# Five instead of four of the eight pairs of the first double unit in the seven-product form, with their first-layer weight sums read where they are made and whole weights stored

## The chip, the cores and the metric

The kernel runs on one core of a Trainium2 chip. The metric is device time in microseconds (us), the median of three runs. The engines are PE (TensorE, matrix products), DVE (VectorE), ACT (ScalarE), POOL (GpSimd) and SP (SyncE, which issues every DMA of this kernel); each runs its own instructions in order and waits for the others by semaphores. SBUF is the memory on the chip, PSUM the banks into which PE accumulates, DRAM the memory behind the DMA queues.

## The reference

```python
ret = scores * Dmat                 # scores = q k^T / 8, Dmat[i, j] = gamma_h ** (i - j) for i >= j, 8 heads of 64, 8 x 576 tokens
x = (ret @ v) -> tokens x 512       # 4608 tokens, heads side by side
h = x @ w_in                        # 512 -> 2048 (first layer)
g = np.maximum(h, 0) + np.log1p(np.exp(-np.abs(h)))   # softplus
out = g @ w_out                     # 2048 -> 512 (second layer)
```

The two weight matrices arrive as 64-bit numbers, the rest as 32-bit.

## The kernel before

**Arithmetic.** Every operand of a large matmul is kept as a high part and a rest (HI, LO), and a product is three matmuls (`TERMS`): rest by high, high by rest, high by high. One such matmul is 128x512 with 128 rows contracted.

**Units.** The 4608 tokens are nine units of 512. Unit 0 is the *opening*: a loop over i = 0 to 15, where one of the 16 slices of the hidden dimension is computed (`hidden_mm`, L540, 12 matmuls), goes through softplus, and is added to the output of the slice before (`output_terms`, L569, 12 matmuls). The 32 weight pieces (16 of w_in, 16 of w_out, 512 KB each) are loaded in this loop, two for each i, into five buffers `wst`, and converted in five steps: p (ACT, L637), t (DVE, L644) and b (DVE, L650) join the two words of a 64-bit number into one fp32 number, c (ACT, L665) makes the high part, d (DVE, L670) the rest. After d the next load is issued (`weight_dl`), and a converted w_in piece is stored to DRAM (`split`), because SBUF has no room to keep it. The order of the steps in an iteration is written out by hand (`ORDERS`).

**Double units.** Units 1 to 8 are four double units, s = 0 to 3, each of 2x2 blocks in tokens and halves of the contracted dimension. The hidden dimension is eight *pairs* j of slices. Done plainly, a pair has eight block products (six matmuls each) in the first layer and eight in the second. In the *seven-product form* (Strassen's, in Winograd's order) it has seven of each: `full_pair` makes the seven of the first layer, and the second layer's are spread over `second` and a later phase. This form needs sums of weight blocks, S1 to S4 for each layer, and sums of x blocks (T1, T2, T3, NT4). The weight sums are made once, in the first double unit, by DVE and ACT: `combine_whole` (L729) or `ring_sum` (L738) add high part and rest to the whole number, `combine_blocks` (L756, four 128x256 additions) makes the sums, `combine_head` (ACT, L760) and `combine_rest` (DVE, L764) split them again, and SP stores them to `combined` (first layer) or `outcombined` (second layer). `whole_out` (L743) makes the whole second-layer weights. From then on all blocks, plain ones and sums, come back from DRAM through a ring of eight buffers, 256 KB a time (`block_load`); `product` (L914) pops one and asks for the next.

**The first double unit** (s = 0) is mixed: pairs 0 to 3 (`MIXED`) have the seven-product form, pairs 4 to 7 (`PLAIN`) are done plainly, as eight *plain slots* (`plain_slot`) for its left half of tokens ahead of the mixed pairs (u = 1) and eight for the right half behind them (u = 2). While the first slots run, weight sums for the mixed pairs are made; in the slots of u = 2 and at the beginning of s = 1, those for pairs 4 to 7. What helpers run in which place is written out in tables of one-letter names (`FIRST_WORK`, `PAIR_WORK`, `SECOND_WORK`, `SUM_WORK`).

**Retention.** Tokens are handled in 36 chunks; one *chunk group* on PE is some 112 to 128 matmuls of 64x64 (`chunk_products`, L236, L252, L340, L352). `GROUPS` puts them into the opening, and the slots and pairs take one each. DVE then scales the values (L294, L498), and helpers add up the T blocks (L506, L517 to L520, L525). `pad()` puts no-ops on PE behind some matmuls, so that instruction blocks end where the chunk groups do (`PADS`).

## Time and profile before

| | |
|---|---|
| median of three runs | 809.93 us (808.10 to 810.88) |
| the profiled execution | 808.64 us, of which the span from first to last instruction 806.9 us |
| PE busy | 800.3 us, 99%, 7228 matmuls, granted clock 1.000 |
| DVE busy | 563.1 us, 70% |
| ACT busy | 398.4 us, 49% |
| DMA | 216.78 MB, 269 GB/s mean |
| the chain that ended last | PE 95%, DMA 3%, DVE 1% |

The opening lasts from about 28 to 120 us of the span, the first slots to 167, the mixed pairs to about 237, the second slots to 286, and the second double unit begins at about 311. Busy shares are means over stages with different limits, so the windows and waits below are taken for one stage each. PE works in a pipeline: the duration of one matmul in a row is longer than the time from one to the next, so that its price is read from the length of a run of many.

### The profile page before, as it was taken

Reading aid. Unit: us, or ns where it says so; the run is one execution under the profiler, and the core shown is the slowest. Engines: PE = TensorE matmul, PEld = TensorE weight load, DVE = VectorE, ACT = ScalarE, POOL = GpSimd, SP = SyncE. Lnnn points to the kernel's source line nnn. Section 1 sums busy time; section 2 is a strip of 40 time slices with the busy share of each in tenths; the row PEclk is TensorE's granted clock in tenths of the full one; section 3 lists DMA queues with packets and bytes.
Section 4 is the critical chain, followed back from the end, with each engine's and each line's share of the span. In section 5 each row is a group of like instructions: output and inputs, shape, how many; then the busy total and the mean of one; then the engine's idle time right before and its main releaser. Section 6 shows DMA issues by size and latency. Waiting matters only on the chain.

```text
span 806.9 us, 19514 instructions
## 1 busy us (share of the span) xinstructions
PE 800.3 (99%) x7228; PEld 659.3 (82%) x7228; DVE 563.1 (70%) x955; ACT 398.4 (49%) x698; POOL 114.1 (14%) x210
## 2 busy tenths in 40 slices
PE   8999999999999999999999999999999999999998
PEld 6788888878888888888888888888888888888887
DVE  5988968688679986667579964546579933224785
ACT  6877763344534363343445644343355734435553
POOL 4322132211221310122111001111100000000000
PEclk9999999999999999999999999999999999999999
DMA  9999879998996779897987678777656775666674
GB/s 358 381 328 331 304 265 381 319 355 292 367 353 214 278 268 395 281 326 255 316 270 234 217 244 258 230 250 252 213 181 218 221 247 192 195 191 194 195 219 159
DMA packets 100458, 216.78 MB, mean 269 GB/s; under 512 B 11152, under 2 KB 11408, under 8 KB 100368
## 3 DMA queue, kind: packets, MB, share of 16 engines
q1 hardware_dynamic: 100368, 215.54, 78.9%
q8 instruction: 62, 1.02, 0.5%
q14 instruction: 28, 0.23, 0.1%
HBM read 174.60 MB, written 40.89 MB: 267 GB/s over the span
## 4 chain that ended last, share of the span: by engine, by line
PE 95%; DMA 3%; DVE 1%; SPq 0%; issue 0%; DVEq 0%
PE sum L1050 20%; PE acc L914 18%; PE third L914 11%; PE two L914 9%; PE two L1050 6%; PE y L569 5%; PE y L580 5%; PE h L540 5%; PE third L252 2%; PE acc L1050 2%; PE third L1050 2%; PE y L1050 2%; PE two L236 2%; PE two L340 2%; PE two L352 2%; DMA wst<-w 1%
## 5 line engine op out<-in xcount | busy, mean ns | idle before, releaser
L1044 DVE TENSOR_TENSOR parts<-g,parts 128x512 fp32r<-128x512 f32 x196 | 134.9, 698 | 138.3 <-ACT parts L1040 135.7
L1050 PE MATMUL sum<-parts,ring 128*128 128x512 f32 x708 | 170.9, 392 | 0.0
L1040 ACT CAST parts<-g 128x512 fp32r<-128x512 f32 x196 | 121.1, 622 | 74.2 <-DVE parts L1044 28.1
L914 PE MATMUL acc<-xt,ring 128*128 128x512 f32 x624 | 156.8, 389 | 0.0
L1050 PEld LDWEIGHTS sum<-parts,ring 128*128 128x128 f32 x708 | 131.6, 188 | 27.8
L914 PEld LDWEIGHTS acc<-xt,ring 128*128 128x128 f32 x624 | 117.0, 188 | 24.4
L914 PE MATMUL third<-xt,ring 128*128 128x512 f32 x408 | 102.7, 389 | 0.0
L914 PEld LDWEIGHTS third<-xt,ring 128*128 128x128 f32 x408 | 76.5, 188 | 16.4 <-DVE s L330 0.3
L914 PE MATMUL two<-xt,ring 128*128 128x512 f32 x336 | 85.7, 390 | 0.7 <-DVE xt L525 0.7
L914 PEld LDWEIGHTS two<-xt,ring 128*128 128x128 f32 x336 | 62.9, 188 | 14.6 <-DVE xt L525 1.1
L229 POOL TENSOR_TENSOR qv<-qv,consts_sb 128x256 f32<-128x256 f32 x58 | 43.4, 748 | 152.9 <-DMA qv<-others 152.9
L1082 ACT COPY acc<-third 128x512 f32<-128x512 f32 x28 | 16.0, 570 | 97.0 <-PE third L914 97.0
L1050 PE MATMUL two<-parts,ring 128*128 128x512 f32 x216 | 50.4, 389 | 0.0
L580 PE MATMUL y<-g,wout 128*128 128x512 f32 x192 | 47.6, 395 | 0.0
L1050 PEld LDWEIGHTS two<-parts,ring 128*128 128x128 f32 x216 | 40.5, 188 | 8.5
L1069 ACT ACTIVATE g<-g 128x512 f32<-128x512 f32 x56 | 35.1, 627 | 23.3 <-DVE g L1102 22.7
L540 PE MATMUL h<-xt,win 128*128 128x512 f32 x192 | 46.1, 390 | 0.0
L569 PE MATMUL y<-wout,g 128*128 128x512 f32 x180 | 44.0, 393 | 0.0
L1125 ACT ACTIVATE g<-acc 128x512 f32<-128x512 f32 x28 | 16.7, 598 | 55.2 <-PE acc L914 55.2
L540 PEld LDWEIGHTS h<-xt,win 128*128 128x128 f32 x192 | 35.9, 188 | 7.7 <-ACT xt L476 0.2
L580 PEld LDWEIGHTS y<-g,wout 128*128 128x128 f32 x192 | 35.4, 188 | 7.9 <-DVE g L555 0.3
L569 PEld LDWEIGHTS y<-wout,g 128*128 128x128 f32 x180 | 33.3, 188 | 7.4 <-ACT g L551 0.3
(168 smaller groups left out, 1262.2 us busy)
## 6 DMA issues: line engine op xcount, KB each, us to landing
ring<-split SPq DMA_DIRECT2D x116, 256.0 KB, 4.4
ring<-combined SPq DMA_DIRECT2D x112, 256.0 KB, 3.5
ring<-outcombined SPq DMA_DIRECT2D x112, 256.0 KB, 3.1
ring<-outsplit SPq DMA_DIRECT2D x84, 256.0 KB, 3.5
qv<-others SPq DMA_DIRECT2D x58, 320.0 KB, 5.3
wst<-w SPq DMA_DIRECT2D x32, 512.0 KB, 6.5
keys<-others SPq DMA_DIRECT2D x58, 256.0 KB, 5.2
split<-win SPq DMA_DIRECT2D x16, 512.0 KB, 6.3
```

The lines of the kernel that those rows point to most:

```text
L229: nc.gpsimd.tensor_mul(v, v, f.unsqueeze(2).broadcast_to([P, 4, D]))
L236: nc.tensor.matmul(L["S"][rows[t], h, part[s]], L["k"][rows[h], s, part[t]], L["q"][rows[h], s, part[t]], start=True, stop=True, skip_grou ...
L252: mm = nc.tensor.matmul(L["T"][rows[h ^ s], t, part[s]], L["kp"][rows[t], s, rows[h]], L["v"][rows[t], s, rows[h]], start=True, stop=True, ...
L540: nc.tensor.matmul(h, tile_of(wins[p], a, kt), xt[:, b, T1 + half, kt % 2], start=(n == 0), stop=(n == 3 * NKT - 1))
L569: nc.tensor.matmul(ys[u][tt], g[:, a, tt * P:(tt + 1) * P], wouts[p][:, :, b], start=p == 0 and n == 0, stop=False)
L580: nc.tensor.matmul(ys[u][tt], tile_of(wouts[p], a, tt), g[:, b], start=u == 1 and p == 2 * MIXED and n == 0, stop=n == 2, skip_group_check ...
L914: nc.tensor.matmul(bank, w[:, ta, kt * P:(kt + 1) * P], xt[:, tb, x, kt], start=start and k == 0, stop=k == 5, skip_group_check=True)
L1040: nc.scalar.copy(t[:, HI], g_slot(J, n))
L1044: nc.vector.tensor_sub(t[:, LO], g_slot(J, n), t[:, HI].bitcast(F32))
L1050: nc.tensor.matmul(bank[m], w[:, a, m * P:(m + 1) * P], t[:, b], start=start and n == 0, stop=n == 2, skip_group_check=True)
L1069: nc.scalar.activation(c, c, AF.Softplus)
L1125: nc.scalar.activation(c21, acc, AF.Softplus)
```

## The change

`PLAIN` goes from 4 to 3: pairs 0 to 4 now have the seven-product form in the first double unit, and six slots are left ahead of them and six behind.

- A permutation `PLACE` decides which buffer and which piece a pair has: the mixed pairs take pieces 6 to 15, and pieces 0 to 5 are the plain ones.
- In the opening, step b writes the joined numbers of a piece side by side, and for the ten w_in pieces of the mixed pairs SP stores them whole (`split_whole`, 256 KB each, right behind b). `combine_load` reads these back instead of high part and rest, so that `combine_whole` is not needed for pairs 0 to 4.
- The first-layer sums of pairs 0 to 4 are written into tiles `direct`, in the SBUF places of the next pair's second-layer weights, and PE reads them there (`product(..., here=...)`) in s = 0. They are stored to `combined` too, for the later double units.
- The first-layer sums of pairs 5 to 7 are made in s = 1 (`load_there`, `combine_whole_of`, `split_store`) and no longer from the ring in the slots of u = 2.
- One chunk group moves from the slots of u = 1 into the opening (`CHUNKS`, `GROUPS`); the work tables and the pads are written anew.

```diff
-PLAIN = 4
+PLAIN = 3
 MIXED = NJ - PLAIN
+PLACE = [(p + 2 * PLAIN) % NF for p in range(NF)]
...
-GROUPS = {1: (4, None), 4: (5, 4), 8: (6, 5), 12: (7, 6), 15: (8, 7)}
-ODD = 12
+GROUPS = {1: (4, None), 4: (5, 4), 7: (6, 5), 10: (7, 6), 13: (8, 7), 15: (9, 8)}
+ODD = 10
+RING_AT = 13
...
+    split_whole = {PLACE[p]: dram.tile([P, 2, HPIECE], F32, name=f"splitwhole{p}") for p in range(2 * MIXED)}
...
-        nc.vector.scalar_tensor_tensor(hi, hi, 3, lo, op0=ALU.logical_shift_left, op1=ALU.bitwise_or)
+        nc.vector.scalar_tensor_tensor(joined(wl[n]), hi, 3, lo, op0=ALU.logical_shift_left, op1=ALU.bitwise_or)
+        p, second = PIECES[n]
+        if not second and p in split_whole:
+            nc.sync.dma_start(split_whole[p], halves(wl[n]))
+
+    def joined(piece):
+        return piece.rearrange("p c a -> p (c a)")[:, 0:PIECE]
...
-            nc.sync.dma_start(f[a], split[2 * j + a].bitcast(F32))
+            nc.sync.dma_start(f[a][:, :, HI], split_whole[PLACE[2 * j + a]])
...
-    def product(bank, x, start=False):
-        w = coming.pop(0)
+    def product(bank, x, start=False, here=None):
+        w = coming.pop(0) if here is None else here
...
-        block_load()
+        if here is None:
+            block_load()
...
+        def sum_here(b):
+            return None if s else direct[J][(b - S1) // 2][:, b % 2]
+
         product(y, B11, True)
         nc.scalar.copy(acc, y)
-        product(z, T1, True)
+        product(z, T1, True, sum_here(S1))
...
-        product(acc, T2)
+        product(acc, T2, here=sum_here(S2))
...
-        product(acc, T3)
+        product(acc, T3, here=sum_here(S3))
...
-        product(z, B22)
+        product(z, B22, here=sum_here(S4))
...
+    def load_there(j, *at):
+        raws[j] = [blocks_in(spare[n]) for n in at]
+        for a, f in enumerate(raws[j]):
+            queued.append(lambda a=a, f=f: nc.sync.dma_start(f, split[PLACE[2 * j + a]].bitcast(F32)))
...
+    def sums_place(j, a):
+        if a not in direct.setdefault(j, {}):
+            p = PLACE[2 * j + 2 + a]
+            place, tag = (wout_pools[p], f"w{p}") if j < MIXED - 1 else (later["quad"], "quad")
+            direct[j][a] = blocks_in(place.tile([P, 2, T], F32R, tag=tag, name="direct"))
+        return direct[j][a]
+
+    def sums_head(j, a):
+        nc.scalar.copy(sums_place(j, a)[:, :, HI], raws[j][a][:, :, LO])
+
+    def sums_rest(j, a):
+        to = sums_place(j, a)
+        nc.vector.tensor_sub(to[:, :, LO], raws[j][a][:, :, LO], to[:, :, HI].bitcast(F32))
+
+    def sums_store(j, a):
+        nc.sync.dma_start(sums_dram[j][a].bitcast(F32), sums_place(j, a).bitcast(F32))
...
-    blocks = schedule((0, prepare_ring, 4, 0, 2))
-    rings = schedule((0, prepare_ring, 4, 2), *[(2 * j - 1, prepare_ring, 4 + j) for j in range(1, 4)])
     for p in range(2 * PLAIN):
         group = groups.pop() if p % 2 else None
-        plain_slot(2, p, B12, B22, group, blocks.get(p, ()), rings.get(p, []) + work_of(SECOND_WORK[p]))
+        plain_slot(2, p, B12, B22, group, (), work_of(SECOND_WORK[p]))
```

The first place is SP in the middle of the opening, about i = 6 to 9: `wst<-w` are the loads of weight pieces, `split<-win` the stores of converted ones. Before:

```order
L627 DMA wst<-w 128x1024 x2
L675 DMA split_116<-win_877 128x1024
L627 DMA wst<-w 128x1024 x2
L675 DMA split_117<-win_956 128x1024
L627 DMA wst<-w 128x1024 x2
```

The same stretch of the change:

```order
L634 DMA wst<-w 128x1024
L660 DMA splitwhole_126<-wst 128x512
L634 DMA wst<-w 128x1024
L688 DMA split_116<-win_850 128x1024
L634 DMA wst<-w 128x1024
L660 DMA splitwhole_127<-wst 128x512
L634 DMA wst<-w 128x1024
L688 DMA split_117<-win_906 128x1024
```

Between the two loads of an iteration now stands a store that reads a `wst` buffer, so that this buffer comes free when the store has landed.

The second place is DVE at the end of the first slots, where it makes the last x sums (L517 to L520, then L525 into `xt`), which the first mixed pair's second product waits for. L555 is the rest of g of the last slot, L756 and L764 weight sums. Before:

```order
L756 TENSOR_TENSOR quad<-quad 128x256 x4
L506 TENSOR_TENSOR xt<-xs,xt 128x2x128
L517 TENSOR_TENSOR xs<-xs 128x2x128
L518 TENSOR_TENSOR t_2659<-xs 128x256
L519 TENSOR_TENSOR xs<-xs 128x2x128
L520 TENSOR_TENSOR xs<-xs,t_2659 128x2x128
L764 TENSOR_TENSOR quad<-quad 128x2x256 x2
L555 TENSOR_TENSOR g<-ab,g 128x512
L525 TENSOR_TENSOR xt<-xs,xt 128x6x128
L525 TENSOR_TENSOR xt<-t_2659,xt 128x2x128
```

The same rows of the change (all line numbers are larger, L562 for L555, L532 for L525):

```order
L513 TENSOR_TENSOR xt<-xs,xt 128x2x128
L524 TENSOR_TENSOR xs<-xs 128x2x128
L525 TENSOR_TENSOR t_2344<-xs 128x256
L526 TENSOR_TENSOR xs<-xs 128x2x128
L527 TENSOR_TENSOR xs<-xs,t_2344 128x2x128
L562 TENSOR_TENSOR g<-ab,g 128x512
L532 TENSOR_TENSOR xt<-xs,xt 128x6x128
L532 TENSOR_TENSOR xt<-t_2344,xt 128x2x128
```

The four additions and the two subtractions of weight sums no longer stand ahead of the last x sums.

The third place is DVE right behind, in the first mixed pair: L743 makes whole second-layer weights of the next pair, L1102 the addition that the pair's c22 needs. Before:

```order
L729 TENSOR_TENSOR quad<-quad 128x2x256 x2
L743 TENSOR_TENSOR quad<-wout_176 128x2x256
L743 TENSOR_TENSOR quad<-wout_177 128x2x256
L756 TENSOR_TENSOR quad<-quad 128x256 x8
L1102 TENSOR_TENSOR g_2733<-acc,g_2733 128x512
```

The change (L755 for L743, L1126 for L1102, L1330 the rest of a sum in its `direct` place):

```order
L768 TENSOR_TENSOR quad<-quad 128x256 x2
L776 TENSOR_TENSOR quad<-quad 128x2x256 x2
L768 TENSOR_TENSOR quad<-quad 128x256 x4
L776 TENSOR_TENSOR quad<-quad 128x2x256
L755 TENSOR_TENSOR quad<-wout_504 128x2x256
L755 TENSOR_TENSOR quad<-wout_505 128x2x256
L1330 TENSOR_TENSOR direct<-quad,direct 128x2x256
L768 TENSOR_TENSOR quad<-quad 128x256 x2
L776 TENSOR_TENSOR quad<-quad 128x2x256
L1126 TENSOR_TENSOR g_2418<-acc,g_2418 128x512
```

The whole weights now stand behind nine rows of sums and splits, and four more operations stand between them and the addition for c22.

## Rows read from the trace of the kernel before

**Rows 1.** Windows: engines' busy us (instructions), PEclk, DMA share, GB/s.
```profile
20.00:40.00 20.00, 19.65 (x140) 15.57 (x138) 18.67 (x36) 16.71 (x30) 6.59 (x10) 1.00 1.00 380
40.00:60.00 20.00, 20.00 (x192) 16.58 (x191) 17.71 (x32) 15.89 (x30) 5.48 (x9) 1.00 0.94 336
60.00:80.00 20.00, 20.00 (x208) 16.59 (x207) 16.38 (x30) 15.71 (x29) 4.03 (x7) 1.00 0.93 322
80.00:100.00 20.00, 20.00 (x208) 16.58 (x207) 18.18 (x33) 15.05 (x28) 2.96 (x6) 1.00 0.86 303
100.00:120.00 20.00, 20.00 (x192) 16.56 (x191) 13.49 (x22) 14.25 (x26) 6.27 (x10) 1.00 0.80 273
...
340.00:360.00 20.00, 20.00 (x192) 16.59 (x191) 11.93 (x21) 9.40 (x17) 3.06 (x6) 1.00 0.95 325
```

**Rows 2.** The chain in order of time: start us, us, what (opening).
```profile
31.17 2.72 PE h L540 x12
...
44.93 0.20 PE third L252
...
46.95 2.95 PE y L569 x12
```

**Rows 3.** The chain: second slots, and the beginning of s = 1.
```profile
238.39 2.95 PE y L580 x12
241.34 1.60 PE y L1050 x6
...
286.46 2.91 PE y L580 x12
...
312.55 1.65 PE two L914 x6
```

**Rows 4.** Timeline of PE at the first mixed pair: start us, us, operation.
```profile
168.90 0.61 PE L914 MATMUL two<-xt,ring 128*128 128x512 f32 x2
170.21 1.19 PE L914 MATMUL two<-xt,ring 128*128 128x512 f32 x4 [0.69 <-DVE xt L525]
```

**Rows 5.** Timeline of DVE ahead of that product.
```profile
166.97 1.29 DVE L764 TENSOR_TENSOR quad<-quad 128x512 fp32r<-128x512 f32 x2
168.18 0.69 DVE L555 TENSOR_TENSOR g<-ab,g 128x512 fp32r<-128x512 f32 x1
168.78 1.37 DVE L525 TENSOR_TENSOR xt<-xs,xt 128x768 fp32r<-128x768 f32 x1
```

**Rows 6.** Timeline of ACT: the high part of that g.
```profile
167.01 0.62 ACT L551 CAST g<-ab 128x512 fp32r<-128x512 f32 x1
```

**Rows 7.** Timeline of DVE in the first mixed pair.
```profile
174.72 0.69 DVE L743 TENSOR_TENSOR quad<-wout 128x512 f32<-128x512 f32 x1 [1.26 <-DMA outcombined<-quad]
...
179.69 0.69 DVE L1102 TENSOR_TENSOR g<-acc,g 128x512 f32<-128x512 f32 x1 [1.10 <-PE acc L914]
```

**Rows 8.** DVE lines by form: busy us, mean ns, idle us before them.
```profile
L756 DVE TENSOR_TENSOR quad<-quad 128x256 f32<-128x256 f32 x64 | 27.1, 445 | 1.2
...
L644 DVE TENSOR_SCALAR wst<-wst 128x512 int32<-128x512 uint32 x32 | 15.3, 482 | 0.3 <-DMA wst<-w 0.3
...
L729 DVE TENSOR_TENSOR quad<-quad 128x512 f32<-128x512 f32 x8 | 6.2, 812 | 0.0
```

**Rows 9.** DMA issues: KB each, median us to landing.
```profile
combined<-quad SPq DMA_DIRECT2D x16, 512.0 KB, 4.1
outcombined<-quad SPq DMA_DIRECT2D x16, 512.0 KB, 6.1
```

**Rows 10.** Timelines of ACT, PE and DVE in the opening.
```profile
85.73 0.62 ACT L551 CAST g<-ab 128x512 fp32r<-128x512 f32 x1 [0.29 <-DVE ab L547]
...
87.35 2.88 PE L569 MATMUL y<-wout,g 128*128 128x512 f32 x12
...
86.99 0.69 DVE L670 TENSOR_TENSOR win<-wst,win 128x512 fp32r<-128x512 f32 x1
...
88.72 0.69 DVE L670 TENSOR_TENSOR wout<-wst,wout 128x512 fp32r<-128x512 f32 x1 [0.70 <-ACT wout L665]
```

More of the change, by code (lines that the diff above doesn't have):

```diff
@@ L43 @@
 STEPS1 = 14
-CHUNKS = 9
+CHUNKS = 10
 FIRST_HALF = NF // 2
@@ L91 @@
 SPLITS = 4
-SEQUENCE = tuple((k, J) for k, js in ((2, range(4)), (1, range(2)), (3, range(4)), (1, range(2, 4)), (4, range(4)))
-                 for J in js)
+SEQUENCE = tuple((k, J) for k, js in ((2, range(MIXED)), (1, range(2)), (3, range(MIXED)), (1, range(2, MIXED)),
+                                      (4, range(MIXED))) for J in js)
 LATE = 7
@@ L579, in output_mm @@
             if u:
-                nc.tensor.matmul(ys[u][tt], tile_of(wouts[p], a, tt), g[:, b], start=u == 1 and p == 2 * MIXED and n == 0,
+                nc.tensor.matmul(ys[u][tt], tile_of(wouts[PLACE[p]], a, tt), g[:, b], start=u == 1 and p == 2 * MIXED and n == 0,
                                  stop=n == 2, skip_group_check=True)
@@ L681, in weight_dl, with pair_blocks @@
             weight_store(n)
-    def pair_blocks(j):
-        blocks = [(j, b) for b in ORDER_PAIR]
+    def pair_blocks(j, kinds=ORDER_PAIR):
+        blocks = [(j, b) for b in kinds]
         return blocks[:-1] + [(j - 1, A12, True)] * (j > 0) + blocks[-1:] + [(j, A11, True)]
     plain = [(j, b) for j in range(MIXED, NJ) for b in range(A22 + 1)]
-    order = plain + [x for j in range(MIXED) for x in pair_blocks(j)]
-    for j in range(MIXED):
-        order += plain[j * 4:j * 4 + 2] + [(MIXED - 1, A12, True)] * (j == 0)
-        order += plain[j * 4 + 2:j * 4 + 4] + [(j, PHASE[0][0], True)]
+    order = plain + [x for j in range(MIXED) for x in pair_blocks(j, (A11, A12, A22))]
+    for p in range(2 * PLAIN):
+        order += plain[2 * p:2 * p + 2] + [(MIXED - 1, A12, True) if not p else (p - 1, PHASE[0][0], True)]
     order += [(J, PHASE[k][0], True) for k, J in SEQUENCE]
@@ L880, in retention_softplus_ffn @@
                 block_load()
+        for j in STORES.get(i, ()):
+            p = PLACE[2 * j]
+            nc.sync.dma_start(wout_dram[2 * j][:, 0].bitcast(F32), wouts[p][:, 0].bitcast(F32))
+            nc.sync.dma_start(wout_dram[2 * j + 1].bitcast(F32), wouts[p + 1].bitcast(F32))
         if i:
@@ L951, in plain_slot @@
             scale_values(k)
-        if u == 2 and p % 2:
+        if u == 2 and p:
             second(ys[2][:2], t)
@@ L956, in plain_slot @@
         outputs_of(u, 2 * MIXED + p)
-    raws = {}
+    raws, direct = {}, {}
     def prepare(j):
@@ L1229, in start, with combine_whole_of, split_store @@
         combined_x([tmps[i][:, n] for n in range(4)], column(i), nc.vector)
+    def load_there(j, *at):
+        raws[j] = [blocks_in(spare[n]) for n in at]
+        for a, f in enumerate(raws[j]):
+            queued.append(lambda a=a, f=f: nc.sync.dma_start(f, split[PLACE[2 * j + a]].bitcast(F32)))
+    def combine_whole_of(j):
+        combine_whole(raws[j])
+    def split_store(j):
+        combine_split(raws[j])
+        for where, f in zip(sums_dram[j], raws.pop(j)):
+            queued.append(lambda where=where, f=f: combine_store([where], [f]))
     def whole_there(j, at):
@@ L1352, in retention_softplus_ffn @@
             if s == FULL:
-                job(divmod(13, NJ), start, 1)
+                for i in range(2):
+                    job(divmod(2 + 11 * i, NJ), start, i)
             else:
```

76 lines of the change are left out of this document (44 added, 32 removed), and 3 rows, old and new, of the table PAIR_WORK.

## The prediction

> **What bounds the kernel now.** I read the busy time by windows first, then the chain, and then the timelines of the engines around the few places where PE does not run through. In the windows PE stands at 20.00 us of 20 from 40 us on [rows 1], and the chain lies on PE for 95% of the span, so what PE has to do is nearly all of the time. What a matmul costs is read from the chain: twelve of 128x512 take 2.72 us [rows 2], so 0.227 us each. PE loses time in two ways only. One is small and regular: a chunk group takes 2.02 us from its first matmul to the next large one, and the run of twelve behind it 2.95 in place of 2.72 [rows 2]; the same 2.95 stands behind a group in a slot [rows 3]. A group costs about 2.25 us wherever it stands, so moving one from the slots into the opening changes nothing by itself. The other way is a late x sum or weight sum, which DVE makes. At the first mixed pair two of six matmuls ran at 168.90, the third was due 0.45 later at 169.35 and came at 170.21, with DVE named as the releaser: 0.86 us lost [rows 4]. Runs that are longer than their matmuls need stand at 241.34 (1.60 for 1.36), 286.46 (2.91 for 2.72) and 312.55 (1.65 for 1.36) [rows 3]: 0.24, 0.19 and 0.29. Together 1.6 us can be had from late DVE work, no more.
>
> **The change part by part.**
>
> *Matmuls.* A plain pair has eight products of six matmuls in each layer, a seven-form pair seven. One pair changes form in one double unit: 2 x 6 = 12 matmuls fewer, at 0.227 [rows 2] **-2.7 us**. PE is the chain there, so this is saved in full if nothing else comes late. Reading a sum in `direct` instead of in a ring buffer changes only an address for PE: at 0, between these bounds: nothing at the low end, and one late first weight load, which I price with the later waits. 21 ring loads of 256 KB that fall away are SP and DMA work; no PE wait on them is in the rows, so 0.
>
> *The last x sums.* Before, L555 stands behind the second of two L764 and begins at 168.18; L525 begins 0.60 later [rows 5]. L555 needs the high part that ACT ends at 167.01 + 0.62 = 167.63 [rows 6]. With the weight sums moved ahead or behind, L555 can begin at 167.65 and L525 at 168.25, 0.5 us earlier. The loss of 0.86 becomes about 0.35. It can't be worse than before by this edit, and at best, with L525 shorter than the 1.37 of its row, nothing is lost: -0.3 to -0.86, taken as **-0.5**.
>
> *DVE in the second slots.* For pairs 4 to 7 sixteen ring sums, sixteen L756 and eight L764 leave these slots: at 0.445 for the 256-wide ones [rows 8] and 0.645 for L764 (two take 1.29) [rows 5], 32 x 0.445 + 8 x 0.645 = 19 us. The three late runs of 0.24, 0.19 and 0.29 stand there or right behind [rows 3]. They are 0.72 us in all; since pair 4's own sums come into the first unit at the same time, I take most, not all: **-0.6** (0 to -0.72). What is moved comes back in s = 1: six L729 at 0.81, twelve L756, six L764, less the second-layer work of pair 4, is 14 - 4.5 = 9.6 us of DVE. In s = 1 DVE was busy 11.93 of 20 us [rows 1], and the pairs of s = 1 take some five such windows, so 8 us of idle time a window cover it: 0. Without this cover it would cost up to 9.6.
>
> *The opening's stores.* Ten stores of 256 KB and one more group's loads (two steps of 576 KB) come into the opening, 3.8 MB. SP issues each between the two weight loads of an iteration, and the buffer that it reads is free only when it has landed. So loads that went out behind the d step of a w_in piece (DVE L670, ends 86.99 + 0.69 = 87.68) go out behind that of the w_out piece (88.72 + 0.69 = 89.41) [rows 10]: 1.7 us later at the worst. Before, DVE waited 0.3 us for these loads over all 32 [rows 8]. Of a late load PE sees nothing up to 1.0 us, because the high part of g is done at 85.73 + 0.62 = 86.35 and PE takes it at 87.35 [rows 10]; in an iteration with a chunk group there are 2.25 us more. That leaves up to 0.7 us in each iteration without a group near it, of which the new `GROUPS` leaves three (5, 8 and 11): 0 to 2.1, taken nearer to the row of 0.3, as **+0.5**.
>
> *Waits on stores behind the first pairs.* In pair 0 the whole second-layer weights of the next pair take buffers that the stores to `outcombined` read. Before, L743 waited 1.26 us there for such a store, and behind it L1102 still waited 1.10 us for PE [rows 7]: the wait was covered. In the change four more operations stand between the two, about 0.6 + 0.45 x 2 + 0.6 = 2.1 us, and the pair begins earlier against a store that takes a median of 6.1 us to land [rows 9]. Behind L1126 PE waits with the pair's last product but one. Below: the cover of 1.10 less 1.26 kept as it is, 0; above: 1.26 + 2.1 - 1.10 - 0.6 (earlier sums) = 1.7. I take **+0.4**. In the same way the tiles `direct` of pair 2 lie where pair 3's g is written: ACT's first copies of pair 3 wait until the two 512 KB stores of these sums have landed, 4.1 us after their issue [rows 9], and they go out at the end of pair 2, with the last six matmuls of pair 2 and twelve of pair 3 ahead of the copy, 18 x 0.227 = 4.1 us. The two are equal; behind a late copy stand the next products' banks. 0 to +1, taken as **+0.3**.
>
> [...]
>
> **Sum.** -2.7 - 0.5 - 0.6 + 0.5 + 0.4 + 0.3 = -2.6 us. The profiled execution of 808.6 (span 806.9) becomes 806.0; the median of the runs lay 1.3 above the profiled one, so 809.9 - 2.6 = **807.3**.
>
> **Rivals.**
> A, the forecast, **807.3**, 805.6 to 808.7 by its terms.
> B, *the waits on stores eat the gain*: both at their upper ends and the opening at 0.5, -2.7 - 1.1 + 0.5 + 1.7 + 1.0 = -0.6: **809.3**. For it: before, DVE already waited at these very stores; against it: it waited with cover.
> C, *the opening becomes bound by its transfers*, on the other side. Three iterations with one group take PE 6 x 2.72 + 2.25 = 18.6 us. They now move 3 x (3 x 512 + 256) KB and 1152 KB of steps, 6.7 MB: 360 GB/s, where the windows show 336, 322 and 303, and 380 in the one window in which the queue was full, share 1.00 [rows 1]. At 380 the stage is fed in 17.6 us. If stores and loads with their waits for buffers only reach 322, three iterations take 20.8 us, 2.2 more, and ten iterations 7.3 us more: -2.7 - 1.1 + 7.3 = +3.5, **813.4**. It decides for slower at about 328 GB/s. Against it: PE was at 20.00 in these windows, so their rates were what was asked for, not what could be had.
> The Trainium skill's page DMA: Bandwidth & Descriptors (Specifications) names about 358 GB/s as the limit of one core's memory; by that the stage would stand just at its bound and rival C would be likelier than I make it. The trace disagrees in one window, with 380.
> D, *all waits vanish*: -2.7 - 0.86 - 0.72 = -4.3, **805.6**.
> That the product count is other than said can't be: the program's rows are written out.
>
> **How the numbers follow.** A 0.48, B 0.23, C 0.18, D 0.11. A difference under 0.3%, 2.4 us, cannot be told from no change in this kernel; 807.5 is that bound, so A stands only just on the faster side, and I give a quarter of A to no change. Faster: 0.36 + 0.11 + a little of B = 0.49; same: 0.12 + 0.2 + a little of C = 0.35; slower 0.16. The range goes from below D, 804.9, into C, 812.0: it leaves out half of C and a little of D.
>
> **What the profile would show.** Right: 7216 matmuls; DVE windows of the second slots clearly below 20; the wait on x sums under 0.4; PE at 20.00 in the opening. Wrong: PE y or h rows over 2.72 in iterations without a group, released by ACT or DVE behind `wst`, with the DMA share at 1.0 (C); PE waits behind L1126 or ACT's copies in pairs 0 and 3 with a store as the releaser (B); or DVE at 20 of 20 in s = 1 with x or weight sums late there. A stall of over 1 us at a place that I name nowhere would make the whole sum wrong.

## The result, and the profile after

The changed kernel takes 815.32 us in the median of seven runs (811.86 to 816.39), the kernel before 809.74 (808.10 to 810.88): a ratio of 1.0065, 95% interval 1.0045 to 1.0084. It is slower by 0.65%. 807.3 was forecast, so 8 us are to be found.

The page of the changed kernel: the span, and busy us, share and instructions of each engine.

```profile
span 813.6 us, 19170 instructions
## 1 busy us (share of the span) xinstructions
PE 802.0 (99%) x7216; PEld 658.2 (81%) x7216; DVE 557.4 (69%) x942; ACT 398.8 (49%) x704; POOL 118.8 (15%) x210
```

The twelve matmuls are gone (7228 to 7216), and yet the span has grown by 6.7 us. The windows of the changed kernel (columns as in [rows 1]) show in which stages PE stood still:

```profile
40.00:60.00 20.00, 20.00 (x192) 16.58 (x191) 17.42 (x31) 15.69 (x30) 5.26 (x8) 1.00 0.94 327
60.00:80.00 20.00, 20.00 (x208) 16.59 (x207) 16.38 (x29) 13.05 (x26) 5.37 (x8) 1.00 0.95 332
80.00:100.00 20.00, 19.10 (x202) 15.28 (x201) 16.93 (x31) 16.02 (x30) 5.23 (x8) 1.00 0.96 344
100.00:120.00 20.00, 19.58 (x308) 16.12 (x307) 14.09 (x25) 12.85 (x23) 5.41 (x10) 1.00 0.98 353
...
200.00:220.00 20.00, 18.41 (x268) 14.76 (x270) 13.23 (x26) 7.54 (x14) 3.76 (x8) 1.00 0.85 299
...
260.00:280.00 20.00, 20.00 (x302) 16.80 (x292) 13.29 (x22) 5.24 (x9) 4.94 (x10) 1.00 0.47 158
...
340.00:360.00 20.00, 17.14 (x174) 13.60 (x173) 14.67 (x27) 6.28 (x11) 3.73 (x7) 0.96 1.00 363
360.00:380.00 20.00, 20.00 (x203) 16.43 (x203) 12.22 (x23) 8.73 (x16) 3.14 (x7) 0.95 0.81 270
```

Against [rows 1] the opening is fuller (344 and 353 GB/s for 303 and 273) and PE no longer runs through in it; PE misses 1.6 us at 200 to 220; and at 340 to 360, at the beginning of s = 1, it misses 2.9 us and its granted clock is below 1 there and in the next window. The second slots, where DVE work was taken out, are as forecast: DVE 13.29 of 20, where the same window of before had 19.72:

```profile
260.00:280.00 20.00, 20.00 (x191) 16.33 (x189) 19.72 (x36) 7.76 (x12) 5.84 (x8) 1.00 0.78 283
```

For a sum I went through PE's rows in order of their starts. Each large matmul should begin 0.227 us behind the one before, or 2.34 us where a chunk group lies between; whatever is more is lost. The usual restart of about 0.11 us behind a group stays in these figures. A loss counts in the stage in which the matmul ahead of it began. In us, by stage of the profiled execution:

```
                        opening  first slots  mixed pairs  second slots  pairs of s=1
                         40-120    120-168      168-240      240-290       315-440
before                     0.45       0.49         1.67         0.71          0.89
after                      2.52       1.20         2.79         0.50          6.47
e1_join_behind_group       4.31       1.22         4.72         0.51          2.96
e2_no_moved_loads          2.26       1.84         4.96         0.51          1.19
e3_spread                  2.30       1.45         4.57         0.51          2.96
e4_no_whole_stores         0.97       0.82         4.94         0.51          7.42
e5_pads_moved              3.42       1.52         1.78         0.50          4.80
e6_stores_early            1.58       1.69         3.49         0.51          3.90
f2_spread_pads_early       2.67       1.24         2.41         0.51          7.14
f3_no_whole_weights        0.96       2.35         5.45         0.51          6.63
f4_spread_no_waits         2.19       1.86         1.90         0.50          1.33
f5_opening_inputs_earlier  1.91       1.85         1.07         0.51          1.45
f6_last_inputs_earlier     1.64       4.72         1.02         0.50          1.57
f7_orders_moved...         0.96       3.61         1.10         0.51          2.27
f8_repaired                1.26       0.92         4.65         0.51          1.45
f9_orders_only             1.28       2.13         2.54         0.51          4.29
f10_repaired_ring_early    1.50       1.30         2.32         0.51          1.45
f11_stores_in_middle       1.37       1.11         0.61         0.50          1.33
```

Between before and after this is +2.1, +0.7, +1.1, -0.2 and +5.6, together +9.3; less the 2.7 of the matmuls that gives 6.6 of the 6.7 us by which the span grew. Each row is one execution, and executions differ: seven of the changed kernel by 4.5 us, seven of the kernel before by 2.8, and 29 of the kernel before, run beside f8, f9 and f10, by 5.4 (807.72 to 813.10). Stages that an edit does not touch show the spread: the last column is 3.9 to 7.4 in the five kernels that have the changed kernel's s = 1 unaltered (after, e4, e5, e6, f9). So a column is compared where an edit acts and against this spread, and times by their ratios.

**The beginning of s = 1.** The chain of the changed kernel there, in order of time:

```profile
348.81 7.56 DMA quad<-split
356.37 0.02 issue
356.40 0.04 DVE quad L741
356.43 0.57 issue
357.01 0.43 DVE u L328
357.44 0.02 issue
357.46 0.43 DVE s L339
357.89 0.04 issue
357.94 2.47 PE third L931 x6
360.41 2.15 PE two L931 x6
362.56 1.36 PE acc L931 x6
```

A 512 KB load of the moved work takes 7.56 us to land. DVE's join of it (L741) waits for it, and behind the join, in DVE's own order, stand L328 and L339 (the two DVE rows of the chain), which read a chunk group's result out of the bank `third`. PE's next product needs that bank. So a transfer that nobody needs for another pair stops PE for 2.1 us. Then six matmuls take 2.47 and 2.15 us in place of 1.36. The granted clock in these microseconds:

```profile
357.00:358.00 1.00, 0.06 (x1) 0.06 (x1) 0.97 (x4) 0.00 (x0) 0.40 (x1) 1.00 1.02 416
358.00:359.00 1.00, 1.00 (x4) 0.81 (x5) 1.00 (x3) 0.00 (x0) 0.62 (x1) 0.76 1.01 395
359.00:360.00 1.00, 1.00 (x4) 0.80 (x3) 0.93 (x4) 0.00 (x0) 0.00 (x0) 0.50 1.04 399
360.00:361.00 1.00, 1.00 (x3) 0.77 (x3) 0.66 (x2) 0.51 (x1) 0.00 (x0) 0.50 0.66 256
361.00:362.00 1.00, 1.00 (x4) 0.74 (x3) 0.00 (x0) 0.06 (x1) 0.00 (x0) 0.54 0.69 235
362.00:363.00 1.00, 1.00 (x6) 0.83 (x5) 0.00 (x0) 0.41 (x1) 0.00 (x0) 1.00 0.96 287
```

After its stop PE runs at 0.50, the lower of its two levels, for some 3.5 us, and eight matmuls lose 0.2 us each.

That DVE was not short of time is seen in one window of 53 us over the first pairs of s = 1. Before:

```profile
312.00:365.00 53.00, 52.98 (x589) 43.34 (x591) 33.51 (x59) 21.84 (x38) 8.76 (x16) 1.00 0.93 317
```

and after:

```profile
312.00:365.00 53.00, 50.10 (x533) 39.99 (x532) 33.17 (x58) 19.47 (x34) 8.46 (x16) 0.97 0.97 353
```

In this window DVE is as busy as before (33.17 and 33.51 us); it stands in front of transfers. Over all pairs of s = 1 (315 to 440 us) it is busy for 88.8 of 125 us, 86.4 before.

**The other places.** The waits of PE in the whole changed kernel (us in total, times, longest):

```profile
PE third L931 <- DVE s L339: 2.1, 1, 2.1
PE third L259 <- issue: 2.1, 2, 1.4
...
PE third L931 <- DVE s L337: 0.7, 1, 0.7
...
PE third L259 <- POOL qv L236: 0.4, 1, 0.4
...
PE acc L931 <- ACT g L1113: 0.2, 1, 0.2
```

The longer of the two stops in the second row lies inside the chunk group of the third mixed pair, with nothing that PE waits for; the other, 0.7 us ahead of a group of the opening at 82.5 us, has no releaser in the trace either. In PE's timeline of the changed kernel:

```profile
203.67 0.22 PE L359 MATMUL two<-qv,s 64*64 64x64 f32 x1
205.28 0.21 PE L259 MATMUL third<-qv,keys 64*64 64x64 f32 x1 [1.39 <-issue]
```

An instruction transfer (queue q8, 16 KB) had begun at 203.01, 0.85 us behind the group's first matmul, and ended at 203.89, 1.39 us before PE went on. In the opening, ACT and DVE wait for weight loads:

```profile
ACT wst L644 <- DMA wst<-w: 3.9, 2, 2.3
...
DVE wst L651 <- DMA wst<-w: 3.0, 6, 0.9
```

which was 0.3 us for DVE before [rows 8]. And ACT's first copy of the fourth mixed pair waits for the store of a sum, in its timeline:

```profile
212.07 0.59 ACT L1108 COPY g<-two 128x512 f32<-128x512 f32 x1 [2.50 <-DMA combined<-direct]
```

### The profile page after: what moved, and what is told of

Its sections match the earlier page's. It is cut to its first block, busy times and chain, and to the rows that moved or that the text cites. A ratio compares the mean times of both kernels' runs of the same rounds, so it can differ in the third digit from the quotient of the medians.

```text
span 813.6 us, 19170 instructions
## 1 busy us (share of the span) xinstructions
PE 802.0 (99%) x7216; PEld 658.2 (81%) x7216; DVE 557.4 (69%) x942; ACT 398.8 (49%) x704; POOL 118.8 (15%) x210
## 4 chain that ended last, share of the span: by engine, by line
PE 85%; DMA 8%; DVE 2%; ACT 2%; issue 1%; SPq 1%; POOL 0%; DVEq 0%; ACTq 0%; POOLq 0%
PE sum L1069 19%; PE acc L931 16%; PE third L931 11%; PE two L931 9%; PE two L1069 7%; PE y L587 4%; DMA wst<-w 3%; PE y L1069 2%; PE third L1069 2%; PE acc L1069 2%; PE third L259 2%; PE y L576 2%; PE two L243 2%; PE h L547 2%; PE two L347 2%; DMA quad<-split 2%
## 5 line engine op out<-in xcount | busy, mean ns | idle before, releaser
L1063 DVE TENSOR_TENSOR parts<-g,parts 128x512 fp32r<-128x512 f32 x203 | 137.7, 690 | 135.4 <-ACT parts L1059 132.9
L1059 ACT CAST parts<-g 128x512 fp32r<-128x512 f32 x203 | 125.4, 622 | 77.5 <-DVE parts L1063 26.6
L931 PE MATMUL acc<-xt,ring 128*128 128x512 f32 x558 | 140.5, 389 | 0.0
L931 PEld LDWEIGHTS acc<-xt,ring 128*128 128x128 f32 x558 | 104.6, 188 | 22.2 <-DVE g L1126 0.4
L931 PE MATMUL two<-xt,ring 128*128 128x512 f32 x288 | 74.1, 393 | 0.0
L931 PEld LDWEIGHTS two<-xt,ring 128*128 128x128 f32 x288 | 54.7, 190 | 12.0 <-DVE held L1315 0.4
L1069 PE MATMUL two<-parts,ring 128*128 128x512 f32 x234 | 54.5, 389 | 0.0
L1069 PEld LDWEIGHTS two<-parts,ring 128*128 128x128 f32 x234 | 43.9, 188 | 9.1
L259 PE MATMUL third<-qv,keys 64*64 64x64 f32 x816 | 34.5, 222 | 2.5 <-issue 2.1
L259 PEld LDWEIGHTS third<-qv,keys 64*64 64x64 f32 x816 | 28.5, 134 | 10.1 <-issue 8.8
```

What stands on the lines that cost most here:

```text
L259: mm = nc.tensor.matmul(L["T"][rows[h ^ s], t, part[s]], L["kp"][rows[t], s, rows[h]], L["v"][rows[t], s, rows[h]], start=True, stop=True, ...
L931: nc.tensor.matmul(bank, w[:, ta, kt * P:(kt + 1) * P], xt[:, tb, x, kt], start=start and k == 0, stop=k == 5, skip_group_check=True)
L1059: nc.scalar.copy(t[:, HI], g_slot(J, n))
L1063: nc.vector.tensor_sub(t[:, LO], g_slot(J, n), t[:, HI].bitcast(F32))
L1069: nc.tensor.matmul(bank[m], w[:, a, m * P:(m + 1) * P], t[:, b], start=start and n == 0, stop=n == 2, skip_group_check=True)
```

## The experiments

Times are medians; ratios are to the kernel before, run on the same chip beside each experiment (its median lay between 808.83 and 809.25 us there, and at 809.74 beside the changed kernel). So two kernels are compared by their ratios; 0.1% is 0.8 us.

### The moved sums in s = 1

**e1_join_behind_group** moves three calls from a place ahead of the chunk group to one behind it:

```diff
-  (("in", 0), combine_whole_of, 5), ... (("in", 1), combine_whole_of, 6), ... (("in", 2), combine_whole_of, 7)
+  (("end", 0), combine_whole_of, 5), ... (("end", 1), combine_whole_of, 6), ... (("end", 2), combine_whole_of, 7)
```

> Only the place of six joins of high part and rest (pairs 5 to 7, second double unit) on DVE changes: behind the chunk group's operations, not ahead of them. In the changed kernel PE loses 6.5 us in the pairs of s = 1 (0.9 before), 2.3 and 0.9 of them where PE's first product of a pair waits for DVE to read the bank third, and DVE waits there for the 512 KB loads that the joins read. Theory (DVE stands in the join, waiting for a load, ahead of work that PE needs): the loss falls by 4 to 5 us, 815.3 becomes 810 to 811.5. Rival 1 (the DMA queue is full there, ring loads come late whatever stands behind them): falls by 1 to 2 us at most. Rival 2 (the 10 us of DVE work that came into s = 1 are too much): no change.

812.71 us, ratio 1.0049 (1.0033 to 1.0065). The loss in s = 1 falls from 6.5 to 3.0, below the spread of 3.9 to 7.4; by the ratio the time falls by 0.16%, 1.3 us, and the intervals overlap (1.0045 to 1.0084 for the changed kernel). The waits at the bank `third` are gone. The gain is below the theory's 4 to 5 because, behind the group, the joins still wait (3.09 us for pair 5's load) and DVE comes late to the addition for c22 (L1126, 0.8 us of PE); it is as late there, 0.65 to 0.94 us, in e4, e5, e6 and f9, whose s = 1 is unaltered.

**e2_no_moved_loads** leaves the loads out:

```diff
 def load_there(j, *at):
     raws[j] = [blocks_in(spare[n]) for n in at]
-    for a, f in enumerate(raws[j]):
-        queued.append(lambda a=a, f=f: nc.sync.dma_start(f, split[PLACE[2 * j + a]].bitcast(F32)))
```

> Leaves out the six loads of 512 KB in s = 1 (the sums of pairs 5 to 7 are then made from whatever lies in the buffers), all DVE, ACT and store work of the moved sums stays. Theory and rival 1 (the loads, by the wait of the join or by filling the queue): loss in the pairs of s = 1 at most 1.5 us, 809.5 to 811. Rival 2 (DVE work): loss stays at 5 to 6.5, 814 to 816.

811.41 us, ratio 1.0034 (1.0021 to 1.0047), 0.31% or 2.5 us below the changed kernel, and 1.2 us lost in s = 1, near the 0.9 of before. The median lies 0.4 above the range that was expected. Its window of the first pairs:

```profile
312.00:365.00 53.00, 52.98 (x557) 43.53 (x556) 36.01 (x63) 21.33 (x38) 8.51 (x15) 1.00 0.93 313
```

DVE is busier (36.01) than in the changed kernel and PE runs through. Rival 2, too much DVE work, is out.

**e3_spread** begins the moved sums in pairs 0, 2 and 4 in place of 0, 1 and 2, joins behind the groups:

> The moved sums of pairs 5, 6, 7 begin in pairs 0, 2 and 4 of s = 1 in place of 0, 1 and 2, with the second-layer sums between them, and the joins stand behind the chunk group. Theory: about the time of the kernel with the joins behind the group alone (810 to 811.5), since the queue was not the limit. Rival 1 (full queue): 2 us or more below that kernel, with DMA share in 320 to 365 us below 0.95 in place of 0.96 to 1.04. Rival 2 (DVE work): somewhat better than the changed kernel, 812 to 814.

812.79 us, ratio 1.0045 (1.0028 to 1.0062): as e1, with the same 3.0 us lost in s = 1; both medians lie 1.2 to 1.3 us above the range that was expected. The queue was hardly less crowded than in e1 (DMA share 0.97 in 320 to 365 us, 1.00 in e1, and not below 0.95), so this run says little about rival 1; f4 below does. What was left is in pair 1: pair 5's join, at the end of pair 0, still waits 2.76 us for its load, and L1126 is late behind it.

### The opening, and the whole weights

**e4_no_whole_stores** takes out the store behind step b and loads high halves only:

```diff
-        if not second and p in split_whole:
-            nc.sync.dma_start(split_whole[p], halves(wl[n]))
...
-            nc.sync.dma_start(f[a][:, :, HI], split_whole[PLACE[2 * j + a]])
+            nc.sync.dma_start(f[a][:, :, HI], split[PLACE[2 * j + a]][:, :, HI].bitcast(F32))
```

> Leaves out the ten stores of whole weights in the opening; the sums of pairs 0 to 4 are made from the high parts alone, loaded from the pieces that are stored anyway (256 KB each as before, so the weights' rests are left out of the sums). In the changed kernel PE loses 2.5 us between 40 and 120 us (0.45 before), and ACT and DVE wait 3.9 and 3.0 us for weight loads (0.2 and 0.3 before). Theory (the stores hold buffers and fill the queue): this loss falls to 0.8 or less, the time by 1.5 to 2.2 us, to 813.1 to 813.8. Rival (it comes from the chunk group that was moved into the opening, with its 1.2 MB of loads): falls by 0.5 at most.

812.41 us, ratio 1.0048 (1.0029 to 1.0068), by the ratio 0.17% or 1.4 us below the changed kernel, within the intervals, with 1.0 us lost in the opening in place of 2.5, and no wait of ACT or DVE for weight loads between 40 and 120 us. The theory holds for the stage, where it had said 0.8 or less.

**f9_orders_only** moves two entries of the written orders of conversion steps:

```diff
-    9: ('d1', 'abs', 't3', 'c2', 'states', 'loads', 'd2', 't4', 'p4', 'exp', ...
+    8: ('d1', 'abs', 't3', 'c2', 'states', 'loads', 'd2', 't4', 'p4', 'exp', ...
-    13: ('d1', 'abs', ...
+    11: ('d1', 'abs', ...
```

> The changed kernel with the written orders at i = 5, 8 and 11 and nothing else. Theory (half of the opening's loss is the misplaced orders): PE's loss between 40 and 120 us falls from 2.5 to 1 to 1.5; the time falls by about 1 us within the scatter of this kernel, 813.5 to 815. Rival (only the stores count): loss stays at 2 to 2.7.

812.41 us, ratio 1.0035 (1.0017 to 1.0052), lower than was expected; 1.3 us lost in the opening, and 0.6 more at 40 us, just ahead of the stage. So stores and orders are not two shares of one sum: with either repair two losses of the changed kernel, 0.75 us in the group at i = 10 and 0.4 two iterations further on, are not seen. The stores make loads late (DVE still waits 2.8 us for them here), and the likely reason why PE sees it is the order left at i = 9 and 13, with late steps ahead of g. It is not fully shown: f7, f8, f10 and f11, which have the orders moved too, lose nothing in that group either, but nor do e6, f5 and f6, which have the old orders and the stores.

### The stop in the chunk group, and the stores behind pair 2

**e5_pads_moved** is one entry of a table:

```diff
-PADS = {..., 10: 64, 12: 28, 17: 98, ...}
+PADS = {..., 10: 64, 11: 28, 17: 98, ...}
```

> Only the 28 no-ops that stood behind the chunk group of the third mixed pair are put ahead of it (behind the group before), so that the group lies 28 instructions later against the blocks in which PE's instructions are fetched; all else is as in the changed kernel. In four of the five kernels profiled so far PE stopped in this group for 1.3 to 2.2 us with nothing that it waits for, and in one of them the releaser was not named; an instruction transfer was under way. Theory (the group uses up its instructions before the next block has come): this stop of 1.7 us (up to 3.1 in other runs) goes, 815.3 becomes 812.5 to 813.7. Rival (it is one more late transfer of retention's inputs): the stop stays, no change.

813.44 us, ratio 1.0048 (1.0029 to 1.0066), as expected, though the interval overlaps that of the changed kernel. PE shows no stop in this group; the loss in the mixed pairs is 1.8 for 2.8. Twenty-eight no-ops at another place and nothing else: the theory stands, and the other traces bear it out. In the seven kernels with the no-ops in the old place (after, e1 to e4, e6, f9) PE stops at the same instruction (4,801 of its own stand ahead of it) and goes on 1.3 to 1.5 us after a 16 KB instruction transfer has ended. In six of them this transfer begins 0.9 to 2.1 us behind the group's first matmul, and the stop takes 1.3 to 2.3 us; in f9 it begins 0.5 us ahead of it, and the stop takes 0.15. In the ten kernels with the no-ops moved the transfer begins 8 to 10 us ahead of the group, and no such stop is seen.

**e6_stores_early** issues the two stores of pair 2's sums at its beginning and middle:

```diff
-("o3 h3 D2 E2 S3 r3", "l3 m3 t3", "w4", "V3 H3 R3 s4", "T2 F2 L4 D3 E3")
+("T2 o3 h3 D2 E2 S3 r3", "l3 m3 t3", "w4 F2", "V3 H3 R3 s4", "L4 D3 E3")
```

> Only the two stores of the third mixed pair's sums from their places in SBUF are issued earlier, at the beginning and the middle of that pair in place of its end. In the changed kernel ACT's first copy of the fourth pair waits 2.5 us for their landing and PE loses 0.36 behind it (0.7 to 1.7 in the other kernels). Theory: ACT no longer waits, PE's loss at this place is under 0.1, the time falls by 0.4 to 1.0 us, to 814.3 to 814.9. Rival (ACT is late for another reason): no change there.

815.82 us, ratio 1.0079 (1.0053 to 1.0105), no gain in the median. ACT's wait at the fourth pair and PE's loss behind it are gone as expected; 0.8 us was lost at 168 us, in the first mixed pair, where a wait for another store came through:

```profile
167.03 0.69 DVE L755 TENSOR_TENSOR quad<-wout 128x512 f32<-128x512 f32 x1 [2.41 <-DMA outcombined<-quad]
```

```profile
167.76 0.62 ACT L1326 CAST direct<-quad 128x512 fp32r<-128x512 f32 x1 [4.88 <-DVE quad L755]
```

Behind L1326 in ACT's order stands the copy L1113, which PE waits for. Whether the early stores made this wait longer is not shown.

### Together

**f2_spread_pads_early** has the pads, the early stores, and the moved work spread, with pair 5's second-layer join at `("in", 0)`:

> The no-ops moved, the stores issued earlier, and the moved sums of pairs 5 to 7 spread over s = 1 with the joins behind chunk groups and, for pair 5, one pair later, so that no join waits for its load. From the losses that PE shows in the changed kernel (2.5 in the opening, 1.7 in the group, 0.4 at the store, 6.5 in s = 1, of which 0.9 are the groups' own): -5.3 - 1.7 - 0.4 = -7.4, 807.9; with the scatter of the opening 807.5 to 809.5, at or just below the kernel before. If the queue itself stays the limit in s = 1: 809.5 to 811.

814.42 us, ratio 1.0060 (1.0044 to 1.0076): a miss, and an instructive one. DVE's timeline of this kernel:

```profile
326.06 1.29 DVE L755 TENSOR_TENSOR quad<-wout 128x512 f32<-128x512 f32 x2 [4.30 <-DMA out<-quad]
```

and PE's:

```profile
328.20 2.07 PE L931 MATMUL third<-xt,ring 128*128 128x512 f32 x4 [2.86 <-DVE s L339]
```

The join that I had put there writes buffers from which output blocks are still being stored. It waits 4.30 us, PE stops for 2.86, and the clock is at 0.50 behind it (four matmuls in 2.07 us). It is the same mechanism as in the changed kernel with another transfer, a store in place of a load.

**f3_no_whole_weights** goes back to 512 KB loads and joins for pairs 0 to 4, the rest as f2:

```diff
-            nc.sync.dma_start(f[a][:, :, HI], split_whole[PLACE[2 * j + a]])
+            nc.sync.dma_start(f[a], split[PLACE[2 * j + a]].bitcast(F32))
...
+        if j < MIXED and not first:
+            combine_whole(raws[j])
```

> As f2_spread_pads_early, and the whole weights are not stored: the sums of pairs 0 to 4 are made as in the kernel before, from 512 KB loads and a join on DVE (ten joins of 0.8 us come into the first slots and pairs). Theory (the ten stores cost the opening 1.5 to 2 us, and the first slots have DVE time to spare): 1 to 1.5 us below f2_spread_pads_early, 806.5 to 808. Rival (the joins make the x sums late at the first mixed pairs, and 512 KB loads fill the queue there): equal or up to 2 us above it.

818.21 us, ratio 1.0115 (1.0092 to 1.0138). The opening loses 1.7 us less than in f2, the first slots and mixed pairs 4.2 us more. The rival is right, by more than it said (3.8 us): this part of the change pays for itself.

**f4_spread_no_waits** has f2's pads and stores, and these places for the moved work:

```diff
+(("x", 0), load_there, 5, 0, 1), (("end", 1), combine_whole_of, 5), (("end", 1), prepare_sums, 5), (1, split_store, 5),
+(("y", 1), load_there, 6, 3, 2), (("end", 2), combine_whole_of, 6), (("x", 3), prepare_sums, 6), (2, split_store, 6),
+(("y", 3), load_there, 7, 0, 1), (("end", 3), combine_whole_of, 7), (("x", 4), prepare_sums, 7), (3, split_store, 7),
+(("in", 4), whole_there, 5, 2), ... (("in", 5), whole_there, 6, 0), ... (("in", 6), whole_there, 7, 2), ...
```

> No-ops moved and stores issued early as before, and the moved work of s = 1 placed so that no DVE operation ahead of a chunk group's reads waits for a transfer: loads of pairs 5, 6, 7 in pairs 0, 1 and 3, joins behind the groups of pairs 1, 2 and 3, the second-layer sums in pairs 4 to 7. Theory (what costs is DVE standing in front of a transfer, not the bytes): PE loses at most 1.5 us in the pairs of s = 1 (6.5 in the changed kernel), 1.8 to 2.4 in the mixed pairs (2.8), 2.5 in the opening as before; in all 7 us less, 808 to 809.5. Rival (the queue is the limit in s = 1): 2 to 3 us are still lost there, 810 to 811.5.

809.99 us, ratio 1.0016 (1.0004 to 1.0029), half a microsecond above the range. The loss in s = 1 is 1.3 us. f2 and f4 differ in these places alone, and their intervals do not overlap: 0.44%, 3.6 us. In its first pairs the queue is as full as in the changed kernel (DMA share 0.97 in both windows; 338 GB/s, 353 there and 317 before), and PE runs through, which is against rival 1:

```profile
312.00:365.00 53.00, 52.98 (x574) 43.38 (x576) 34.03 (x59) 21.60 (x38) 7.94 (x16) 1.00 0.97 338
```

**f5_opening_inputs_earlier** changes `LOADS` 13 to 12 for steps 18 and 19, and `RING_AT` from 13 to 14:

> As f4_spread_no_waits, and in the opening the inputs of the last chunk group are loaded at i = 12 in place of 13, and the first seven ring loads (1.8 MB) issued at i = 14 in place of 13. In the changed kernel and most others PE loses 0.4 to 1.75 us in the last group of the opening, with the landing of its qv inputs as the cause (7.1 us after the issue). Theory: this loss goes, 0.4 to 1.5 us below f4_spread_no_waits, 807 to 808.5. Rival (the weight loads behind take the delay instead, since the queue is full there): no difference.

809.48 us, ratio 1.0008 (0.9993 to 1.0023). PE loses nothing in the opening's last group here, as expected; the time is 0.5 lower, which is no more than scatter, and above the range of 807 to 808.5.

**f6_last_inputs_earlier** also changes `LOADS` 15 to 14 for steps 20 and 21:

> As f5_opening_inputs_earlier, and the inputs of the group in the first plain slot are loaded at i = 14 of the opening in place of 15, ahead of the ring loads. In f4_spread_no_waits and f5_opening_inputs_earlier PE loses 0.9 and 0.5 us in one of the first groups of the slots, with POOL waiting for qv. Theory: this goes, 0.3 to 0.7 us below f5_opening_inputs_earlier, 808.8 to 809.2. Rival (the ring loads behind come late instead): no difference.

812.53 us, ratio 1.0040 (1.0025 to 1.0055): a miss. PE waits 2.5 us for the first ring load of the slots, which now stands on SP behind these inputs. The rival named it.

**f7_orders_moved_with_groups** is f6 with f9's edit:

> As f6_last_inputs_earlier, and the hand-written orders of conversion steps that belong to the iterations behind a chunk group stand at i = 5, 8 and 11, behind the groups at 4, 7 and 10, where the change left them at 5, 9 and 13. In the changed kernel the step p of a late weight piece stands ahead of ACT's work on g, and PE loses 0.4 us at i = 11 and up to 1.2 us in the group at 10. Theory (the orders no longer fit the groups): the loss in the opening falls from about 2 to 1 us or less, 0.5 to 1.5 us below f6_last_inputs_earlier. Rival (the loads are late whatever the order is): no difference.

811.14 us, ratio 1.0032 (1.0019 to 1.0045). The opening loses 1.0 us where f6 loses 1.6; the ring load is still 1.7 us late.

**f8_repaired** is f5 with f9's edit, and **f10_repaired_ring_early** the same with `RING_AT = 13`:

> f5_opening_inputs_earlier (no-ops moved, stores early, s = 1 spread, inputs of the opening's last group earlier) with the written orders of conversion steps at i = 5, 8, 11. The ring loads stand where f5 had them, so that the 1.7 to 2.5 us that PE lost to a late ring load in f6 and f7 do not come back. Theory: the opening loses about 1 us in place of 1.9, all else as in f5: 808.3 to 809, 0 to 0.1% below the kernel before (809.0). Rival (orders do nothing, f7's opening was chance): as f5, 809.5.

> As f8_repaired, with the first ring loads at i = 13 as in the changed kernel. Theory: they stand ahead of the inputs of the first slot's group and behind those of the opening's last one, and nothing is late in the slots: equal to f8_repaired or up to 0.5 us below it. Rival (1.8 MB earlier in the full queue): 0.5 to 1 us above it.

808.21 us, ratio 0.9990 (0.9975 to 1.0005), and 808.23, ratio 0.9989 (0.9972 to 1.0007). They can't be told from one another, nor from the kernel before. In the profiled execution of f8 the third pair's group waits 1.8 us for POOL's work on qv, which is not so in f10; both have the stores of pair 2 early.

**f11_stores_in_middle** is f10 with these stores behind the B22 product:

```diff
-("T2 o3 h3 D2 E2 S3 r3", "l3 m3 t3", "w4 F2", "V3 H3 R3 s4", "L4 D3 E3")
+("o3 h3 D2 E2 S3 r3", "l3 m3 t3", "w4", "V3 H3 R3 s4 T2 F2", "L4 D3 E3")
```

> f10_repaired_ring_early with the two stores of the third pair's sums issued behind its B22 product, a third of a pair ahead of where the changed kernel has them and half a pair behind where f10 has them. Theory (early stores make the group's inputs late): no loss over 0.3 us at 198 to 204 us of the span, and ACT's wait at the fourth pair stays covered; 0.5 to 1 us below f10, 807.2 to 807.8, and below the kernel before beyond the interval. Rival (the lateness there has nothing to do with these stores): as f10, 808.2, or above it where ACT waits again.

807.55 us, ratio 0.9983 (0.9973 to 0.9993): below the kernel before, beyond the interval, and with 806.24 to 808.78 without the scatter of the others. Its interval overlaps those of f8 and f10, so that the gain over them is not shown by the times. Its page and all of PE's waits in it:

```profile
span 805.0 us, 19166 instructions
```

```profile
PE idle L806 <- DVE fill L788: 1.5, 1, 1.5
PE pair L420 <- DMA raw<-whole: 0.5, 1, 0.5
PE third L259 <- DVE ab L554: 0.3, 1, 0.3
```

Only waits of the beginning are left. The span is 2.0 us below that of before: 2.7 for the matmuls, 1.1 in the mixed pairs and 0.2 in the second slots, against 0.9 in the opening, 0.6 in the first slots, 0.4 in the pairs of s = 1 and some 0.2 behind them.

## Why the prediction was wrong

*Matmuls, -2.7.* Right: 7216, and f11 shows that they can be had. (Of the ring loads 14 fell away by the pages, 424 to 410, and not 21; no PE wait on one is among the waits of the changed kernel, so the term stays at 0.)

*The last x sums, -0.5, and the second slots, -0.6.* The first is right: the first mixed pair's second product loses 0.2 us in the changed kernel, 0.86 before. Of the second only 0.2 came. The 0.29 at the beginning of s = 1 is there as before, in all kernels, so it was no effect of the second slots' load on DVE.

*What is moved into s = 1, 0.* This is the step that failed, with 5.6 of the 9.3 us in the profiled execution (3.0 to 6.5 in the five profiles with this stage unaltered). I wrote that eight idle us a window on DVE cover 9.6 us of work. The window that I took, 11.93 of 20, is one of the emptiest of the stage (340 to 360; 360 to 380 has 15.06), but the time was there: in e2 DVE does all this work, 93.9 of 125 us, and PE runs through. I did not count the loads and stores of the moved step, and above all I treated idle time as if an operation could use any of it. DVE takes its instructions in order. A join that waits for a 512 KB load, 7.6 us from issue to landing, keeps DVE from the two reads behind it, and those hold PE's bank. e2 (no loads, DVE busier, 1.2 us lost) and f4 (all loads, queue as full, joins where their loads have landed, 1.3 us lost) show it from both sides, and f2 shows it with a store. The price in the profiled execution was 3.2 us for the two longest stops (0.9 and 2.3), 1.6 for the clock behind the second, and small ones. At the first of the two the joins themselves no longer wait; DVE is late from a wait of 4.15 us for a moved load ten us before.

*The opening, +0.5.* Mis-sized: +2.1. The buffers do come free later, as the step said, but I took the margin of 1.0 us from one iteration of the kernel before, three behind a group, and gave it to all. The orders written for i = 9 and 13 stayed there while the groups moved to 7, 10 and 13, which the diff shows by not touching them. f9 and e4, each with one of the two repaired, suggest that either alone would have cost little. Another part, 0.65 us, is the opening's last group, which waits for its own inputs (qv); the term counted their loads and gave them no price. Rival C, the opening bound by its transfers, gave nearly the time that was measured, for the wrong reason: f11 moves all these bytes and loses 1.4 us there. The Trainium skill's limit of some 358 GB/s (DMA: Bandwidth & Descriptors, Specifications), which is what two cores share divided by two, is not where this kernel on one core stops: f11 has windows of 372 and 375 GB/s with PE at 19.86 and 20.00 of 20.

*Stores behind the first pairs, +0.4 and +0.3.* The second is right in place and size (ACT waits 2.50 us, PE loses 0.36). Of the first nothing is seen in the changed kernel (L755 waits 1.02 and 0.51 us for stores, and PE loses nothing behind it), and 0.8 us in e6, by another way than the step said: not through L1126, but through ACT's L1326 and the copy behind it.

*What was not named.* The 0.7 us of the first slots are small losses, the largest 0.3 at 120.7 us; f11 keeps 0.6 of them. The larger one is the stop in the third pair's group, 1.7 us. I had dismissed the place of groups against the blocks of instructions ("a group costs about 2.25 us wherever it stands"); the change rewrote the table of no-ops that sets it, and by a count in the trace 4,602 instructions of PE stand ahead of this group, and 4,630 to 4,632 with the no-ops moved. The Trainium skill (Runtime: NRT & Kernel Launch, Instruction fetch mechanics) has instructions arrive in blocks of 256, the cost mostly hidden. The trace agrees on the blocks (60 instruction transfers with 0.98 MB for 15,514 instructions of PE, so that this group begins six ahead of an edge, 18 x 256 = 4608), not on the hiding for a group of 128 small matmuls in 2 us.

Open stays why single executions of one kernel, the changed one or the one before, differ by some 3 to 5 us. Where two profiles of related kernels differ, it is in which transfer is late, and f11, in which no wait on a transfer is left behind the beginning, has the least scatter of those that ran twelve times; that is an indication and no proof.

## What to carry to other kernels

Idle time of an engine that works in order is only worth what stands behind the new instruction: ask of every moved operation which transfer it waits for, when that lands with the queue as full as it will be, and what the same engine has next that the bottleneck needs. Put the operation behind that, or a stage after its load. When stages move, look for tables that are keyed by place and were not moved with them: written orders, no-ops, load times.

## What the runs showed of the hardware that was not expected

A stop of PE of 2 to 3 us can cost more than itself. After 2.1 us the granted clock was 0.50 for some 3.5 us and eight matmuls lost 0.2 us each; after 2.9 us in f2 it was 0.50 for 6 us and thirteen matmuls lost 2.6 us. In f8 it was 0.50 for some 3 us after the 1.8 us that the third pair's group waits for POOL. It need not fall: after a stop of 0.9 us at 340 us no matmul was slow, nor was one after the 2.3 us in the chunk group of e1 (after 2.2 us at the same place in e2 the clock was 0.50), nor after the 2.5 us for a ring load in f6, behind which the clock stood at 1.00. PE's row there, and the microsecond behind it:

```profile
124.75 2.55 PE L931 MATMUL acc<-xt,ring 128*128 128x512 f32 x10 [2.53 <-DMA ring<-split]
```

```profile
125.00:126.00 1.00, 1.00 (x6) 0.83 (x6) 0.00 (x0) 0.00 (x0) 0.00 (x0) 1.00 1.04 402
```

What decides between the two is not shown here.

And PE can stop for 1.3 to 2.3 us in the middle of a run of small matmuls for its instructions alone, which twenty-eight no-ops, put elsewhere, remove.
